# The second softmax's read in 64-row tiles, and W_in chunks and scores moved into one stretch where the accumulators change

## Chip, cores, metric

One core of one Trainium2 chip runs the kernel. The metric is the device time of one execution in microseconds (us), the median of three runs.

## What is computed

Two layers, all in float32. With B = H = 8, S = 512 tokens, Ns = 32 state rows and D = 64:

```python
scores  = scale * x @ state^T            # (B, H, S, Ns), softmax over Ns  -> a
xread   = a @ state                      # (B, H, S, D)
scores2 = scale * state @ x^T            # (B, H, Ns, S), softmax over S   -> a2
sread   = a2 @ x                         # (B, H, Ns, D)
x   = concat([xread, sread], axis=2)     # heads put side by side: 4352 rows of 512
h   = x @ w_in                           # 512 -> 2048
g   = h if h >= 1, 0 if h <= -1, (h + 1)^2 / 4 between
out = g @ w_out                          # 2048 -> 512
```

## The kernel before

**Work per batch.** `b` is a batch, 0 to 7; `b == B` (8) is the tail that handles the 256 rows of `sread`. For b < 8 the kernel never forms `xread`: it multiplies `state` with `W_in` first (`sw`, 128 x 2 x 2048 for one b: rows are head pair and state row, the 2 is the head in its pair), and then h = a x `sw`. `sw` is made in eight chunks of 256 columns; chunk c of batch b serves hidden block j = c.

**Precision.** The large products run on fp32r operands. Each operand is split in a high and a low part, and a product is three matmuls (high x high, low x high, high x low). ACT makes a high part (a cast), DVE the low part (a subtraction). `sw`, the scores and the second softmax's read are plain fp32 matmuls; each of those has two records in the trace.

**Steps.** A step is (b, j), j = 0 to 7. On TensorE it consists of `g1(b, j)`, 12 matmuls 128x512 into two PSUM banks of tag "h", and of `g2` of the step before, 24 matmuls 128x512 into the four banks of tag "acc" (`acc[b][0..3]`, one for each 128 tokens). Between `g1` and its `g2` stands an elementwise chain: `relu` on each half and `square` (ACT), `bound` on each half (DVE, which frees the h banks), `gh` (ACT), `gl` (DVE). In the last `g2` of a batch the pairs are sorted by token block, so a bank is complete after each six matmuls, and `store` copies it out on ACT.

**What is put between.** `g2` of a step is cut after `cut` of its eight triples of matmuls, and other TensorE work stands in the cut: at j = 0 the `scores` of b+1 (tile `sc`) and the second softmax's read of b (`read2`, tile `sr`); at j = 1 a transpose `rt`, at j = 2 the transposes `e2p`; at j = 3 and j = 7 four chunks of `sw` each (`sw_four`, chunks 4 to 7 of b, and chunks 0 to 3 of b+1). For b = 1 chunk pairs 0, 1 (at the end of a planned prologue) and 2, 3 (at j = 1, `sw_make`) are made in stretches of their own. These matmuls use part of the array: `sw` and `sc` 64 rows x 32 columns, eight such tiles in turn, `sr` 128 rows x 32 columns, four in turn.

**PSUM.** Eight banks: four "acc", two "h", one pair "mm" (used by `sc`, `rt`, `e2p`, half of `sw_four`).

**Order.** Batch 0 is emitted by a planner (`Plan`) with costs and due times. From b = 1 on the code above is handed to a scheduler that keeps the data dependences and may reorder within each engine's stream; the order views below show the result. The loads `xt` (for the scores) and `xn` (for the read) go through SP's queue, one buffer each, and are issued when the previous user is done.

Of the kernel before, what the change touches and what calls it, by code (L numbers as in the profile page):

```python
# [8 lines left out]
F32 = mybir.dt.float32  # L9
# [4 lines left out]
ALU = mybir.AluOpType  # L14
# [8 lines left out]
class Plan:  # L23
# [13 lines left out]
    def op(self, key, engine, cost, run, after=(), take=(), ends=()):  # L37

        after = list(after)
        prior = self.last.get(engine) if engine in ("PE", "SP") else None  # L40
        self.last[engine] = key
        self.ops[key] = [engine, cost, run, after, list(take), list(ends), prior]
# [95 lines left out]
def state_exchange_moe(  # L138
# [17 lines left out]
    nc = tc.nc  # L156
    B, P, NT, H, D = x.shape
    S = NT * P
    NS = 32
    DM = H * D  # L160
    NPR = H // 2
    CI = 256
# [3 lines left out]
    NJ = NF // 2  # L166
# [4 lines left out]
    small = ctx.enter_context(tc.tile_pool(name="small", bufs=1))  # L171
# [6 lines left out]
    def ps_acc(name):  # L178
        return ps.tile([P, DM], F32, tag="acc", bufs=4, name=name)

    def ps_h(name):
        return ps.tile([P, 512], F32, tag="h", bufs=2, name=name)

    def ps_mm(name):
        return ps.tile([P, 2, 512], F32, tag="mm", bufs=1, name=name)
# [18 lines left out]
    sb = const.tile([P, B, NPR, NS], F32, name="sb")  # L204
    srT = const.tile([P, NPR, B, NS], F32, name="srT")
    w32 = [const.tile([P, NPR, CI], F32, name=f"w32_{c}") for c in range(NC)]
# [7 lines left out]
    def load_xt(b):  # L214
        xt = work.tile([P, 2, NPR, S // 2], F32, tag="xt", bufs=1, name=f"xt{b}")
        for i in range(2):
            nc.sync.dma_start(out=xt[:, i], in_=xt_in[b, i])
        return xt
# [6 lines left out]
    class Attention:  # L225
# [116 lines left out]
        def read2(self):  # L342
            b = self.b
            xn = loaded.pop(("xn", b))
            sr = ps_h(f"sr{b}") if b else ps_mm(f"sr{b}")[:, 0]
            sr = self.sr = sr[:, :2 * D].rearrange("p (q d) -> p q d", q=2)
            for q in range(2):
                for t in range(NT):
                    for pr in range(NPR):
                        c0 = t * P + pr * NS  # L350
                        nc.tensor.matmul(  # L351
                            sr[pr * NS:(pr + 1) * NS, q], lhsT=self.e2[:, q, c0:c0 + NS],
                            rhs=xn[:, t, 2 * pr + q], start=t == 0, stop=t == NT - 1,
                        )

        def scale2(self):
            b = self.b
            self.rs = small.tile([P, 2, D], F32, tag="rs", name=f"rs{b}")
            nc.vector.tensor_tensor(
                out=self.rs, in0=self.sr, in1=self.r2[:, :, None].broadcast_to([P, 2, D]), op=ALU.mult  # L360
            )

        def keep2(self):
# [33 lines left out]
    def split_tiles(name):  # L397
        hi = work.tile([P, 1024], F32R, tag="wh", name=f"{name}h")
        lo = work.tile([P, 1024], F32R, tag="wl", name=f"{name}l")
        return hi, lo  # L400

    chunk = {}
# [3 lines left out]
    def sw_product(b, c, n):  # L406

        pt = ps_mm(f"sw{b}_{c}")
        for i in range(n):
            for pr in range(NPR):  # L410
                for hh in range(2):
                    rows = slice(hh * 64, hh * 64 + 64)
                    nc.tensor.matmul(
                        pt[pr * NS:(pr + 1) * NS, hh, i * CI:(i + 1) * CI],
                        lhsT=sb[rows, b, pr], rhs=w32[c + i][rows, pr], start=True, stop=True,
                    )
        w = n * CI
        wh, wl = (
            v[:, :2 * w].rearrange("p (q f) -> p q f", q=2) for v in split_tiles(f"sw{b}_{c}")
        )  # L420
        sw_of[b, c] = pt[:, :, :w], wh, wl
        for i in range(n):
            cols = slice(i * CI, (i + 1) * CI)
            chunk[b, c + i] = wh[:, :, cols], wl[:, :, cols]

    def sw_high(b, c):
        pt, wh, _ = sw_of[b, c]
        nc.scalar.copy(out=wh, in_=pt)

    def sw_low(b, c):  # L430
        pt, wh, wl = sw_of[b, c]
        nc.vector.tensor_tensor(out=wl, in0=pt, in1=wh.bitcast(F32), op=ALU.subtract)  # L432

    def sw_make(b, c, n):
        sw_product(b, c, n)
        sw_high(b, c)
        sw_low(b, c)

    def sw_four(b, c):

        pairs = [split_tiles(f"sw{b}_{c + 2 * p}") for p in range(2)]
        wh, wl = ([v.rearrange("p (q f) -> p q f", q=2) for v in w] for w in zip(*pairs))
        own = [ps_h(f"sw{b}_{c}_{hh}") for hh in range(2)]
        both = ps_mm(f"sw{b}_{c + 2}")
        for i in range(4):
            cols = slice(i % 2 * CI, (i % 2 + 1) * CI)
            for pr in range(NPR):
                for hh in range(2):
                    rows = slice(hh * 64, hh * 64 + 64)
                    o = both[:, hh] if i > 1 else own[hh]  # L450
                    nc.tensor.matmul(  # L451
                        o[pr * NS:(pr + 1) * NS, cols], lhsT=sb[rows, b, pr], rhs=w32[c + i][rows, pr],
                        start=True, stop=True,
                    )
            chunk[b, c + i] = wh[i // 2][:, :, cols], wl[i // 2][:, :, cols]
        for hh in range(2):
            h, lo = wh[0][:, hh], wl[0][:, hh]
            nc.scalar.copy(out=h, in_=own[hh])
            nc.vector.tensor_tensor(out=lo, in0=own[hh], in1=h.bitcast(F32), op=ALU.subtract)
        nc.scalar.copy(out=wh[1], in_=both)  # L460
        nc.vector.tensor_tensor(out=wl[1], in0=both, in1=wh[1].bitcast(F32), op=ALU.subtract)

    def wi_split(c):
        wh, wl = (v.rearrange("p (k f) -> p k f", f=CI) for v in split_tiles(f"wj{c}"))
# [117 lines left out]
    parts = {}  # L582
# [49 lines left out]
    op = plan.op  # L632
# [25 lines left out]
    atts = {}  # L658
# [62 lines left out]
    def tensor(key, cost, f, after=(), take=(), ends=()):  # L721
        op(key, "PE", cost, f, after, take, ends)
# [6 lines left out]
    def sw_ops(b, c, n):  # L729
        tensor(("sw", b, c), 0.35 + 0.35 * n, lambda: sw_product(b, c, n), [("w", c + i) for i in range(n)],  # L730
               take=[("mm", ("sw", b, c)), ("w", ("wc", b, c))])
        op(("swh", b, c), "ACT", 0.5 * n, lambda: sw_high(b, c), [("sw", b, c)], ends=[("sw", b, c)])
        op(("swl", b, c), "DVE", 0.6 * n, lambda: sw_low(b, c), [("swh", b, c)], ends=[("sw", b, c)])
# [14 lines left out]
    def g2_ops(b, j, half):  # L748
        k = (b, j)
        tensor(("g2", half) + k, 2.75, lambda: g2(b, j, (4 * half, 4 * half + 4)), [("gh",) + k, ("gl",) + k, ("wol", j), ("sc done", 0)],  # L750
               ends=[("g",) + k])
# [41 lines left out]
    for j in range(NJ):  # L793
# [10 lines left out]
            att_ops2(1)  # L804
        if j:
            g2_ops(0, j - 1, 1)
    sw_ops(1, 0, 2)
    import os
    with guard:
        plan.emit(warm, ("sc", 0, 0), ("g2", 0, 0, 0))  # L810
# [5 lines left out]
    for i, (b, j) in enumerate(steps):  # L816
        if (b, j) == (B, 0):
            sh, sl = (work.tile([P, NPR, B * NS], F32R, tag=t, name=f"s{t}") for t in ("ath", "atl"))
            src = srT.rearrange("p a b n -> p a (b n)")
            nc.vector.tensor_copy(sh, src)  # L820
            nc.vector.tensor_tensor(out=sl, in0=src, in1=sh.bitcast(F32), op=ALU.subtract)
            att_of[B] = (sh, sl)
        if b + 1 < B and j == 0:
            loaded["xt", b + 1] = load_xt(b + 1)
        g1(b, j)
        if i + 1 < len(steps) and steps[i + 1][0] == B:
            for c in (2 * steps[i + 1][1], 2 * steps[i + 1][1] + 1):
                wi_split(c)
        before = steps[i - 1] if i else (0, NJ - 1)
        if b == B:  # L830
            g2(*before)
            continue
        cut = 5
        g2(*before, (0, cut))
        if j == 0:
            if b + 1 < B:
                atts[b + 1] = Attention(b + 1)
                atts[b + 1].scores()
            atts[b].read2()
            atts[b].scale2()  # L840
            if b + 1 < B:
                loaded["xn", b + 1] = load_xn(b + 1)
                atts[b + 1].second()
        elif j == 1:
            atts[b].keep2()
            atts[b].keep()
            if b == 1:
                sw_make(b, 2, 2)
        elif j == 2 and b + 1 < B:
            atts[b + 1].first()  # L850
        elif j == 3:
            sw_four(b, 4)
        elif j == 4 and b + 1 < B:
            atts[b + 1].halves()
        elif j == NJ - 1 and b + 1 < B:
            sw_four(b + 1, 0)
        g2(*before, (cut, 8))
    g2(*steps[-1])

# [42 lines left out]
```

## Time and profile before

| | |
|---|---|
| median of 3 runs | 658.56 us (658.18 to 659.11) |
| the profiled execution: time, span | 658.84 us, 656.8 us |
| TensorE matmul busy | 647.7 us, 99% of the span |
| ACT, DVE busy | 359.6 us (55%), 340.1 us (52%) |
| granted TensorE clock | 1.00 |
| chain that ended last | TensorE 88%, ACT 6%, DVE 4% |

The 2.0 us between time and span lie outside the program's recorded part. Matmuls are pipelined: a record lasts 390 ns, and the next starts 227 ns later. So a busy share of 99% does not say that the array streams without pause; what a stretch costs is read from the starts of the matmuls around it.

### The profile page before, as it was taken

To read this page: it belongs to the slowest core of one execution; us is meant where nothing else is said; L and a number is where in the kernel's file an instruction comes from. 1 tells how busy PE (TensorE), PEld (TensorE's weight loads), DVE (VectorE), ACT (ScalarE), POOL (GpSimd) and SP (SyncE) were. 2 spreads that over 40 slices of the span, in tenths; PEclk is the share of its full clock that TensorE was granted. 3 is DMA by queue.
4 is the path that set the end of the run, shared out by engine and by line. 5 is a ranking of instruction groups with operands and counts; after the bars stand their busy time and mean duration, and the time that the engine had idled before them with its cause. 6 is when DMAs were issued, how large, how long until landed. Compare 5 with 4: busy or idle time off the path is not lost.

```text
span 656.8 us, 10337 instructions
## 1 busy us (share of the span) xinstructions
PE 647.7 (99%) x4442; PEld 518.1 (79%) x4442; DVE 340.1 (52%) x503; ACT 359.6 (55%) x475; POOL 0.8 (0%) x7
## 2 busy tenths in 40 slices
PE   8999999999999999999999999999999999999997
PEld 7677776788787877787787878787787878788895
DVE  5999948433673338533664338434654343333431
ACT  5899847544565455544555456445654454444632
POOL 0000000000000000000000000000000000000000
PEclk9999999999999999999999999999999999999999
DMA  8986005000320005000410005000300000000101
GB/s 355 415 364 244 0 17 177 1 1 1 102 92 1 0 1 193 1 2 1 132 62 1 0 17 177 1 1 1 129 1 1 0 34 32 1 1 1 64 1 32
DMA packets 11085, 43.64 MB, mean 66 GB/s; under 512 B 1312, under 2 KB 1440, under 8 KB 7968
## 3 DMA queue, kind: packets, MB, share of 16 engines
q1 hardware_dynamic: 6096, 34.28, 13.9%
q10 hardware_dynamic: 4944, 8.72, 3.6%
q8 instruction: 34, 0.56, 0.4%
q14 instruction: 11, 0.09, 0.0%
HBM read 34.08 MB, written 8.91 MB: 65 GB/s over the span
## 4 chain that ended last, share of the span: by engine, by line
PE 88%; ACT 6%; DVE 4%; issue 1%; DMA 0%; POOL 0%; ACTq 0%; SPq 0%; POOLq 0%
PE acc L553 18%; PE acc L554 17%; PE acc L555 17%; PE h L498 9%; PE h L499 9%; PE h L497 9%; PE sw L451 4%; PE sr L351 1%; ACT u L502 1%; PE sc L253 1%; PE e2p L333 1%; PE warmed L198 1%; ACT u L505 1%; ACT e L322 1%; ACT raw_i L607 1%
## 5 line engine op out<-in xcount | busy, mean ns | idle before, releaser
L553 PE MATMUL acc<-wo,gh 128*128 128x512 f32 x544 | 216.7, 398 | 0.0
L554 PE MATMUL acc<-wo,gh 128*128 128x512 f32 x544 | 212.4, 390 | 0.0
L555 PE MATMUL acc<-wo,gl 128*128 128x512 f32 x544 | 212.1, 390 | 0.0
L508 DVE SCALAR_TENSOR_TENSOR u<-u,h 128x512 f32<-128x512 f32 x136 | 87.1, 681 | 200.2 <-ACT u L505 200.2
L502 ACT ACTIVATE u<-h,half 128x512 f32<-128x512 f32 x136 | 93.2, 694 | 168.7 <-PE h L499 159.5
L553 PEld LDWEIGHTS acc<-wo,gh 128*128 128x128 f32 x544 | 102.1, 188 | 30.4 <-issue 9.1
L555 PEld LDWEIGHTS acc<-wo,gl 128*128 128x128 f32 x544 | 102.1, 188 | 22.3 <-issue 0.4
L554 PEld LDWEIGHTS acc<-wo,gh 128*128 128x128 f32 x544 | 102.2, 188 | 20.0 <-DVE wo L626 0.3
L522 DVE TENSOR_TENSOR gl<-u,gh 128x1024 fp32r<-128x1024 f32 x68 | 83.2, 1224 | 63.2 <-ACT gh L517 63.2
L517 ACT CAST gh<-u 128x1024 fp32r<-128x1024 f32 x68 | 71.6, 1052 | 70.5 <-DVE u L508 70.3
L505 ACT ACTIVATE u<-u 128x1024 f32<-128x1024 f32 x68 | 72.6, 1067 | 1.5
L568 ACT COPY o<-acc 128x512 f32<-128x512 f32 x33 | 19.0, 583 | 21.3 <-PE acc L555 21.3
L451 PE MATMUL sw<-w,sb 64*32 64x256 f32 x832 | 25.4, 379 | 0.0
L499 PE MATMUL h<-atl,sw_0h 128*128 128x512 f32 x60 | 23.6, 393 | 0.3 <-DVE atl L306 0.2
L498 PE MATMUL h<-ath,sw_2l 128*128 128x512 f32 x60 | 23.5, 391 | 0.2 <-DVE sw_2l L432 0.2
L497 PE MATMUL h<-ath,sw_0h 128*128 128x512 f32 x60 | 23.5, 395 | 0.0
L498 PE MATMUL h<-ath,sw_0l 128*128 128x512 f32 x60 | 23.5, 391 | 0.0
L497 PE MATMUL h<-ath,sw_4h 128*128 128x512 f32 x60 | 23.4, 390 | 0.0
L498 PE MATMUL h<-ath,sw_4l 128*128 128x512 f32 x60 | 23.4, 389 | 0.0
L499 PE MATMUL h<-atl,sw_2h 128*128 128x512 f32 x60 | 23.4, 389 | 0.0
L497 PE MATMUL h<-ath,sw_6h 128*128 128x512 f32 x60 | 23.3, 389 | 0.0
L498 PE MATMUL h<-ath,sw_6l 128*128 128x512 f32 x60 | 23.3, 389 | 0.0
(184 smaller groups left out, 738.1 us busy)
## 6 DMA issues: line engine op xcount, KB each, us to landing
xt<-in_xt_dram SPq DMA_DIRECT2D x16, 512.0 KB, 7.5
raw_i<-in_moe_w_in_dram SPq DMA_DIRECT2D x8, 1024.0 KB, 7.1
raw_o<-in_moe_w_out_dram SPq DMA_DIRECT2D x8, 1024.0 KB, 9.1
xn<-in_x_dram SPq DMA_DIRECT2D x8, 1024.0 KB, 7.3
out_dram<-o ACTq DMA_DIRECT2D x32, 256.0 KB, 2.1
sb<-in_state_dram SPq DMA_DIRECT2D x1, 448.0 KB, 12.5
out_dram<-o SPq DMA_DIRECT2D x4, 64.0 KB, 1.7
out_dram<-o ACTq DMA_DIRECT2D x4, 64.0 KB, 2.0
```

Of the source, the lines that this page charges most:

```text
L451: nc.tensor.matmul(o[pr * NS:(pr + 1) * NS, cols], lhsT=sb[rows, b, pr], rhs=w32[c + i][rows, pr], start=True, stop=True,)
L497: nc.tensor.matmul(o, lhsT=wh[:, k, sl], rhs=ah[:, k], start=first, stop=False)
L498: nc.tensor.matmul(o, lhsT=wl[:, k, sl], rhs=ah[:, k], start=False, stop=False)
L499: nc.tensor.matmul(o, lhsT=wh[:, k, sl], rhs=al[:, k], start=False, stop=last)
L502: nc.scalar.activation(out=self.u[:, i], in_=self.hs[i], func=AF.Relu, scale=0.5, bias=half)
L505: nc.scalar.activation(out=self.u, in_=self.u, func=AF.Square)
L508: nc.vector.scalar_tensor_tensor(out=self.u[:, i], in0=self.u[:, i], scalar=1.0, in1=self.hs[i], op0=ALU.min, op1=ALU.max,)
L517: nc.scalar.copy(out=gh, in_=self.u)
L522: nc.vector.tensor_tensor(out=gl, in0=self.u, in1=gh.bitcast(F32), op=ALU.subtract)
L553: nc.tensor.matmul(a, lhsT=lh, rhs=oh, start=f == 0, stop=False)
L554: nc.tensor.matmul(a, lhsT=lh, rhs=ol, start=False, stop=False)
L555: nc.tensor.matmul(a, lhsT=ll, rhs=oh, start=False, stop=f == NF - 1)
```

## The change

1. `read2` splits the 128 tokens of each contraction in two halves of 64 rows, `g` = 0 and 1, which go to two h banks: 64 matmuls in place of 32, in the tile shape of `sw` and `sc`. `scale2` adds the halves on DVE (a copy, an addition, then the scaling as before).
2. At j = 0 the cut moves behind all of `g2` (8 in place of 5), which finishes the old accumulators. In the cut stand then `read2`, chunks 1 to 4 of `sw`, and `scores`, without other matmuls between. The chunks go into the four acc banks (`ps_acc`), which the stores have just emptied and which `g2(b, 0)` needs next.
3. Chunks 5, 6, 7 of b and 0 of b+1 are made at j = 4, in two h banks and mm. The stretches at j = 3 and j = 7, and `sw_make` at b = 1, go. The prologue makes one chunk of b = 1 in place of two; b = 7 now makes chunks 1 to 7 itself.

```diff
 def read2(self):
-    sr = ps_h(f"sr{b}") if b else ps_mm(f"sr{b}")[:, 0]
-    sr = self.sr = sr[:, :2 * D].rearrange("p (q d) -> p q d", q=2)
+    if b:
+        self.sr = [ps_h(f"sr{b}_{g}") for g in range(2)]
+    else:
+        sr = ps_mm(f"sr{b}")
+        self.sr = [sr[:, g] for g in range(2)]
     for q in range(2):
         for t in range(NT):
             for pr in range(NPR):
                 c0 = t * P + pr * NS
-                nc.tensor.matmul(
-                    sr[pr * NS:(pr + 1) * NS, q], lhsT=self.e2[:, q, c0:c0 + NS],
-                    rhs=xn[:, t, 2 * pr + q], start=t == 0, stop=t == NT - 1)
+                for g in range(2):
+                    rows = slice(g * 64, g * 64 + 64)
+                    nc.tensor.matmul(
+                        self.sr[g][pr * NS:(pr + 1) * NS, q * D:(q + 1) * D],
+                        lhsT=self.e2[rows, q, c0:c0 + NS], rhs=xn[rows, t, 2 * pr + q],
+                        start=t == 0, stop=t == NT - 1)
 def scale2(self):
...
+    nc.vector.tensor_copy(first2, self.sr[0][:, :2 * D])
+    nc.vector.tensor_tensor(out=first2, in0=self.sr[1][:, :2 * D], in1=first2, op=ALU.add)
-    nc.vector.tensor_tensor(out=self.rs, in0=self.sr, in1=self.r2[...], op=ALU.mult)
+    nc.vector.tensor_tensor(out=self.rs, in0=first, in1=self.r2[...], op=ALU.mult)
...
-    sw_ops(1, 0, 2)
+    sw_ops(1, 0, 1)
...
-        cut = 5
+        cut = 8 if j == 0 else 5
         g2(*before, (0, cut))
         if j == 0:
-            if b + 1 < B:
-                atts[b + 1] = Attention(b + 1)
-                atts[b + 1].scores()
             atts[b].read2()
             atts[b].scale2()
+            halves = [
+                sw_pair([(b, c), (b, c + 1)], [ps_acc(f"sw{b}_{c}_{hh}") for hh in range(2)]) for c in (1, 3)
+            ]
-            if b + 1 < B:
+            if nxt:
                 loaded["xn", b + 1] = load_xn(b + 1)
-                atts[b + 1].second()
+                nxt.scores()
+            for split in halves:
+                split()
+            if nxt:
+                nxt.second()
         elif j == 1:
             atts[b].keep2()
             atts[b].keep()
-            if b == 1:
-                sw_make(b, 2, 2)
...
-        elif j == 3:
-            sw_four(b, 4)
-        elif j == 4 and b + 1 < B:
-            atts[b + 1].halves()
-        elif j == NJ - 1 and b + 1 < B:
-            sw_four(b + 1, 0)
+        elif j == 4:
+            last = [(b, 7)] + ([(b + 1, 0)] if nxt else [])
+            own = [ps_h(f"sw{b}_5_{hh}") for hh in range(2)]
+            split = sw_pair([(b, 5), (b, 6)], own)
+            both = ps_mm(f"sw{b}_7")
+            split2 = sw_pair(last, [both[:, hh] for hh in range(2)], both)
+            split()
+            split2()
+            if nxt:
+                nxt.halves()
         g2(*before, (cut, 8))
```

`sw_pair` issues the 16 matmuls of two chunks and returns a function that issues their casts (ACT) and subtractions (DVE). Three places show how the rows move. First TensorE at (b, j) = (2, 0): `acc` rows are `g2(1, 7)`, `h_1` rows are `g1(2, 1)`. Before:

```order
L555 MATMUL acc_2_1078<-wo_781,gl_7_1468 128x512
L253 MATMUL sc_1589<-xt_1540,sb 32x512 x8
L351 MATMUL sr_1601<-xn_1026,e_2_1030 32x64 x32
L553 MATMUL acc_2_1078<-wo_781,gh_7_1467 128x512
L554 MATMUL acc_2_1078<-wo_781,gh_7_1467 128x512
```

Now, the end of the stretch (it begins with the 64 `sr` matmuls and 32 of chunks 1 to 4):

```order
L459 MATMUL sw_3_0_1738<-w_4_91,sb 32x256
L459 MATMUL sw_3_1_1739<-w_4_91,sb 32x256
L253 MATMUL sc_1760<-xt_1585,sb 32x512 x8
L511 MATMUL h_1_0_1792<-ath_984,sw_1h 128x512
L512 MATMUL h_1_0_1792<-ath_984,sw_1l 128x512
```

Nine `g2` matmuls followed the stretch before; now `g1(2, 1)` follows at once, and its second matmul reads the low part of chunk 1, made in this stretch.

DVE at the same place, before (`u` is the elementwise chain's tile, `gl` its last product, `rs` the scaled read, `z` and `nm` the two softmaxes of b+1):

```order
L522 TENSOR_TENSOR gl_0_1564<-u_0_1543,gh_0_1563 128x1024
L260 STREAM_TRANSPOSE z_1590<-sc_1589 128x512 x2
L359 TENSOR_TENSOR rs_1634<-sr_1601,r_2_1191 128x128
L318 TENSOR_REDUCE nm_3_1641<-sc_1589 128x1 x2
L319 TENSOR_SCALAR nm_3_1641<-nm_3_1641 128x1
```

and now:

```order
L536 TENSOR_TENSOR gl_0_1609<-u_0_1588,gh_0_1608 128x1024
L367 COPY first_1714<-sr_0_1647 128x128
L368 TENSOR_TENSOR first_1714<-sr_1_1648,first_1714 128x128
L369 TENSOR_TENSOR rs_1713<-first_1714,r_2_1281 128x128
L473 TENSOR_TENSOR sw_1l<-sw_1_0_1718,sw_1h 128x512
L473 TENSOR_TENSOR sw_1l<-sw_1_1_1719,sw_1h 128x512
L473 TENSOR_TENSOR sw_3l<-sw_3_0_1738,sw_3h 128x512
L473 TENSOR_TENSOR sw_3l<-sw_3_1_1739,sw_3h 128x512
L260 STREAM_TRANSPOSE z_1761<-sc_1760 128x512 x2
```

Two small operations and four subtractions have moved ahead of the softmaxes of b+1. On ACT four casts stand there, behind the last two stores of the old accumulators and ahead of the `relu` of step (2, 1):

```order
L582 COPY o_1620<-acc_2_1189 128x512
L582 COPY o_1620<-acc_3_1190 128x512
L585 DMA out_dram<-o_1620 128x512 x2
L472 CAST sw_1h<-sw_1_0_1718 128x512
L472 CAST sw_1h<-sw_1_1_1719 128x512
L472 CAST sw_3h<-sw_3_0_1738 128x512
L472 CAST sw_3h<-sw_3_1_1739 128x512
L516 ACTIVATE u_1_1791<-h_1_0_1792,half 128x512
```

Before, the exponentials of the second softmax followed the third copy there; they now come behind both `relu`.

More of the change, by code (lines that the diff above doesn't have):

```diff
@@ L350, in read2 @@
                         c0 = t * P + pr * NS
-                        nc.tensor.matmul(
-                            sr[pr * NS:(pr + 1) * NS, q], lhsT=self.e2[:, q, c0:c0 + NS],
-                            rhs=xn[:, t, 2 * pr + q], start=t == 0, stop=t == NT - 1,
-                        )
+                        for g in range(2):
[3 more added lines that the diff above has]
+                                lhsT=self.e2[rows, q, c0:c0 + NS], rhs=xn[rows, t, 2 * pr + q],
+                                start=t == 0, stop=t == NT - 1,
+                            )
         def scale2(self):
@@ L358, in scale2 @@
             self.rs = small.tile([P, 2, D], F32, tag="rs", name=f"rs{b}")
+            first = small.tile([P, 2, D], F32, tag="first", name=f"first{b}")
+            first2 = first.rearrange("p a d -> p (a d)")
+            nc.vector.tensor_copy(first2, self.sr[0][:, :2 * D])
+            nc.vector.tensor_tensor(out=first2, in0=self.sr[1][:, :2 * D], in1=first2, op=ALU.add)
             nc.vector.tensor_tensor(
-                out=self.rs, in0=self.sr, in1=self.r2[:, :, None].broadcast_to([P, 2, D]), op=ALU.mult
+                out=self.rs, in0=first, in1=self.r2[:, :, None].broadcast_to([P, 2, D]), op=ALU.mult
             )
@@ L437, in sw_make, with sw_pair @@
         sw_low(b, c)
[L439 to L446, printed above, removed]
+    def sw_pair(pieces, banks, whole=None):
+        wh, wl = (
+            v.rearrange("p (q f) -> p q f", q=2) for v in split_tiles("sw{}_{}".format(*pieces[0]))
+        )
+        for i, (b, c) in enumerate(pieces):
+            cols = slice(i * CI, (i + 1) * CI)
             for pr in range(NPR):
@@ L449, in sw_four, with split @@
                     rows = slice(hh * 64, hh * 64 + 64)
-                    o = both[:, hh] if i > 1 else own[hh]
                     nc.tensor.matmul(
-                        o[pr * NS:(pr + 1) * NS, cols], lhsT=sb[rows, b, pr], rhs=w32[c + i][rows, pr],
+                        banks[hh][pr * NS:(pr + 1) * NS, cols], lhsT=sb[rows, b, pr], rhs=w32[c][rows, pr],
                         start=True, stop=True,
                     )
[L455 to L461, printed above, removed]
+            chunk[b, c] = wh[:, :, cols], wl[:, :, cols]
+        n = len(pieces) * CI
+        if whole is not None:
+            parts = [(wh[:, :, :n], wl[:, :, :n], whole[:, :, :n])]
+        else:
+            parts = [(wh[:, hh, :n], wl[:, hh, :n], banks[hh][:, :n]) for hh in range(2)]
+        def split():
+            for h, lo, pt in parts:
+                nc.scalar.copy(out=h, in_=pt)
+                nc.vector.tensor_tensor(out=lo, in0=pt, in1=h.bitcast(F32), op=ALU.subtract)
+        return split
     def wi_split(c):
@@ L832, in state_exchange_moe @@
             continue
-        cut = 5
+        nxt = atts[b + 1] = Attention(b + 1) if b + 1 < B and j == 0 else atts.get(b + 1)
+        cut = 8 if j == 0 else 5
         g2(*before, (0, cut))
         if j == 0:
-            if b + 1 < B:
-                atts[b + 1] = Attention(b + 1)
-                atts[b + 1].scores()
             atts[b].read2()
             atts[b].scale2()
-            if b + 1 < B:
+            halves = [
+                sw_pair([(b, c), (b, c + 1)], [ps_acc(f"sw{b}_{c}_{hh}") for hh in range(2)]) for c in (1, 3)
+            ]
+            if nxt:
                 loaded["xn", b + 1] = load_xn(b + 1)
-                atts[b + 1].second()
+                nxt.scores()
[3 more added lines that the diff above has]
+                nxt.second()
         elif j == 1:
@@ L846, in state_exchange_moe @@
             atts[b].keep()
-            if b == 1:
-                sw_make(b, 2, 2)
-        elif j == 2 and b + 1 < B:
-            atts[b + 1].first()
-        elif j == 3:
-            sw_four(b, 4)
-        elif j == 4 and b + 1 < B:
-            atts[b + 1].halves()
-        elif j == NJ - 1 and b + 1 < B:
-            sw_four(b + 1, 0)
+        elif j == 2 and nxt:
+            nxt.first()
+        elif j == 4:
[8 more added lines that the diff above has]
+                nxt.halves()
         g2(*before, (cut, 8))
```

## Prediction

> **What bounds it.** I read the page's busy shares, its chain that ended last, and then the timeline of TensorE around each piece of work that the change touches.
>
> ```profile
> PE 647.7 (99%) x4442; PEld 518.1 (79%) x4442; DVE 340.1 (52%) x503; ACT 359.6 (55%) x475; POOL 0.8 (0%) x7
> PE 88%; ACT 6%; DVE 4%; issue 1%; DMA 0%; POOL 0%; ACTq 0%; SPq 0%; POOLq 0%
> ```
>
> TensorE is the path, so the time is the sum of what its stream takes. The next rows show that stream at (b, j) = (2, 0), where `sc` and `sr` stand between `g2` matmuls, and at (1, 7), where four chunks stand (start, duration, engine, line).
>
> ```profile
> 171.07 0.39 PE L553 MATMUL acc<-wo,gh 128*128 128x512 f32 x1
> ...
> 174.24 0.39 PE L555 MATMUL acc<-wo,gl 128*128 128x512 f32 x1
> 174.56 1.09 PE L253 MATMUL sc<-xt,sb 64*32 64x512 f32 x16
> 175.58 1.10 PE L351 MATMUL sr<-xn,e 128*32 128x64 f32 x64
> 176.61 0.50 PE L553 MATMUL acc<-wo,gh 128*128 128x512 f32 x1
> 176.95 0.40 PE L554 MATMUL acc<-wo,gh 128*128 128x512 f32 x1
> ```
> ```profile
> 163.93 0.39 PE L555 MATMUL acc<-wo,gl 128*128 128x512 f32 x1
> 164.25 1.96 PE L451 MATMUL sw<-w,sb 64*32 64x256 f32 x64
> 166.13 0.50 PE L553 MATMUL acc<-wo,gh 128*128 128x512 f32 x1
> 166.47 0.40 PE L554 MATMUL acc<-wo,gh 128*128 128x512 f32 x1
> ```
>
> From 171.07 to 174.24 are 14 steps: 0.227 us for a full matmul. A stretch costs the time between its outer full matmuls less two such steps (0.45): 176.95 - 174.24 - 0.45 = 2.26 for scores and read, 166.47 - 163.93 - 0.45 = 2.09 for four chunks. Part of that is not streaming. Stretches of one and two chunks show how much:
>
> ```profile
> 68.67 0.66 PE L413 MATMUL sw<-w,sb 64*32 64x256 f32 x16
> 69.26 0.50 PE L553 MATMUL acc<-wo,gh 128*128 128x512 f32 x1
> ...
> 92.09 1.09 PE L413 MATMUL sw<-w,sb 64*32 64x256 f32 x32
> 93.12 0.50 PE L553 MATMUL acc<-wo,gh 128*128 128x512 f32 x1
> ```
>
> One chunk takes 0.59 to the next full matmul, two 1.03, four 1.88: 0.43 a chunk and 0.16 once. Add 0.09 at the entry (0.32 in place of 0.227) and 0.11 behind the first full matmul (0.34 in place of 0.227): 0.36 for each stretch, whatever is in it. `sc` takes 1.02 to the start of `sr`, so 0.86 of streaming and 0.16 for the change of tile shape inside the stretch; `sr` takes 1.03, of which I count 0.89 as streaming and 0.14 as the way out.
>
> **The change part by part.** *Batches 2 to 6.* Before: 2.26 + 2 x 2.09 = 6.44. After, at j = 0: 0.09 + 0.89 (read) + 4 x 0.43 + 0.86 (scores) + 0.27 = 3.83, one tile shape throughout; at j = 4: 2.09. Sum 5.92, saved 0.5 in each, 2.5 in five. What goes is one stretch (0.36) and the change of shape inside another (0.16); the chunks and scores stream as before.
>
> *Batch 1* has more to lose:
>
> ```profile
> 91.77 0.39 PE L555 MATMUL acc<-wo,gl 128*128 128x512 f32 x1
> ...
> 93.45 0.40 PE L554 MATMUL acc<-wo,gh 128*128 128x512 f32 x1
> ...
> 99.25 0.39 PE L555 MATMUL acc<-wo,gl 128*128 128x512 f32 x1
> ...
> 100.87 1.10 PE L351 MATMUL sr<-xn,e 128*32 128x64 f32 x64 [0.21 <-DVE u L508]
> 101.90 0.50 PE L553 MATMUL acc<-wo,gh 128*128 128x512 f32 x1
> ...
> 110.58 0.40 PE L554 MATMUL acc<-wo,gh 128*128 128x512 f32 x1
> ...
> 112.27 0.39 PE L553 MATMUL acc<-wo,gh 128*128 128x512 f32 x1
> ...
> 114.56 0.39 PE L555 MATMUL acc<-wo,gl 128*128 128x512 f32 x1
> 115.17 0.50 PE L498 MATMUL h<-ath,sw_2l 128*128 128x512 f32 x1 [0.23 <-DVE sw_2l L432]
> ```
>
> Two chunks at 91.77 cost 1.23; scores and read 101.90 + 0.34 - 99.25 - 0.45 = 2.54, with a wait of 0.28 for an h bank that `bound` freed late; two chunks of `sw_make` at 110.58 cost 1.24; the wait for their low part 115.17 - 114.56 - 0.23 = 0.38, with the 0.11 behind it 0.5. With two stretches of four chunks 9.7. After: one chunk 0.79, then 3.83 + 2.09 = 6.7. The wait for the h bank goes since the read now follows 19 full matmuls after `g1(1, 0)`, not 6. Saved 3.0.
>
> *Batch 7* pays, since its chunks were made before at (6, 7):
>
> ```profile
> 538.87 0.39 PE L555 MATMUL acc<-wo,gl 128*128 128x512 f32 x1
> ...
> 540.22 0.50 PE L553 MATMUL acc<-wo,gh 128*128 128x512 f32 x1
> 540.56 0.40 PE L554 MATMUL acc<-wo,gh 128*128 128x512 f32 x1
> ```
>
> Before: 540.56 - 538.87 - 0.45 = 1.24, and 2.09. After: 0.09 + 0.89 + 4 x 0.43 + 0.27 = 2.97 without scores, and three chunks 0.36 + 3 x 0.43 = 1.65: 1.3 more, and a wait of 0.4 (below).
>
> *The read in 64-row tiles* is the one unknown. It has 128 records in place of 64, on eight tiles in place of four, and half the contraction each. It streams as now, 0.89, if eight can start in the time in which four start. Its own pace now is one start in (1.10 - 0.22)/63 = 14 ns. But eight tiles do start closer:
>
> ```profile
> 164.25 0.45 PE L451 MATMUL sw<-w,sb 64*32 64x256 f32 x8
> L451 PE MATMUL sw<-w,sb x832: 376/376/400, 129.5 to 566.7; 64*32 64x256 f32 x167
> q8 instruction: 34, 0.56, 0.4%
> ```
>
> These eight of four chunks' 64 ended 0.45 after the first start and last 0.40 at most, so they started 7 ns apart: 128 x 7 = 0.89, just enough. Bounds: 0.86 (a hair faster) to 1.79 (14 ns kept), +0.90 for each of eight reads. I take 0.89, because `sw` is the nearest row in tile shape, eight 64 x 32 tiles that alternate in the same way. Code loading adds a little: 0.56 MB in 34 packets is 16.5 KB each, 256 of TensorE's 8884 records, and 0.4% of 16 x 656.8 us / 34 is 1.2 us for one. A read and the next chunk now use 320 records in about 1.3 us; where a block ends badly TensorE may wait 0.2 to 0.5. I put 0 in the sum and up to 1 us in the range.
>
> *Waits that are new.* `g1(b, 1)` follows the stretch at once and needs chunk 1's high and low parts.
>
> ```profile
> 100.12 1.28 DVE L508 SCALAR_TENSOR_TENSOR u<-u,h 128x512 f32<-128x512 f32 x2 [4.56 <-ACT u L505]
> ...
> 165.43 1.08 ACT L458 CAST sw_0h<-sw 128x512 fp32r<-128x512 f32 x2 [0.24 <-PE sw L451]
> ...
> 166.36 1.28 DVE L459 TENSOR_TENSOR sw_0l<-sw,sw_0h 128x512 fp32r<-128x512 f32 x2
> ...
> 173.55 0.34 ACTq L571 DMA_DIRECT2D out_dram<-o  x1
> 173.99 0.59 ACT L568 COPY o<-acc 128x512 f32<-128x512 f32 x1 [0.47 <-PE acc L555]
> ...
> 176.69 1.31 DVE L260 STREAM_TRANSPOSE z<-sc 128x512 f32<-128x512 f32 x2
> ...
> 177.92 0.26 DVE L359 TENSOR_TENSOR rs<-sr,r 128x128 f32<-128x128 f32 x1
> ...
> 180.59 1.28 DVE L275 TENSOR_TENSOR z<-z,m 128x512 f32<-128x512 f32 x2
> ...
> 186.61 1.23 DVE L522 TENSOR_TENSOR gl<-u,gh 128x1024 fp32r<-128x1024 f32 x1
> ```
>
> Count from the start of the last full matmul. The read starts at 0.32, chunks 1 and 2 end at 0.32 + 0.89 + 0.86 = 2.07, 3 and 4 at 2.93, scores at 3.8, the first full matmul starts at 3.95, the second (low part of chunk 1) at 4.3, the fifth (its other half) at 4.75. The cast follows the end of its stream by 165.43 - 164.25 - 0.86 = 0.32, so at 2.4, and takes 0.55; ACT has the last store behind it by then: a copy starts 0.43 behind the start of its bank's last matmul (the 12th from 171.07, so 171.07 + 11 x 0.227 = 173.56; the copy 173.99), so 0.43 to 1.02, and two DMA issues of 0.34 end at 1.7. DVE, whose additions and scaling (three like L359, 0.26 each) end near 2.3, subtracts from 3.0 to 3.65 and to 4.3; TensorE starts 0.07 behind DVE (100.12 + 0.68 to 100.87). 3.7 and 4.4 against 4.3 and 4.75: covered by the scores, with 0.35 to spare. In batch 7 the scores are missing, the second matmul could start at 3.45 and waits until 3.7: 0.3, and 0.11 for a restart, 0.4. The acc banks are free at 5.5, `g2(b, 0)` needs the first at 6.8. The softmaxes of b+1 start on DVE at 5.5 in place of right behind the scores; from there to L275's end it takes 181.87 - 176.69 - 0.2 = 5.0, the two `bound` 1.3 follow with 0.4 of small work ahead of them (h bank free at 11.6, needed at 12.3), then two sums of L275's size 1.3 and `gl` 1.2: 14.7, needed at 15.5 (24 full matmuls and `g1(b, 2)` behind `g1(b, 1)`). So 0.7 to spare. The loads of `xt` and `xn` pass nothing on SP's queue that is needed within the batch. At j = 4 the casts have the same nine matmuls before their use as at j = 3 before.
>
> *Sum.* -2.5 - 3.0 + 1.3 + 0.4 = -3.8 us. Against the profiled execution's 658.84: 655.0. That execution is 0.28 above the median of the runs, so 654.8 is what I expect of a median.
>
> **Rivals.**
>
> *The read keeps its pace (slower).* If a start each 14 ns is TensorE's limit and not the four tiles', 128 of them take 1.79, and eight reads add 7.2: 654.8 + 7.2 = 662.0. It decides from 3.8/8/128 = 3.7 ns more than 7, that is 10.7 ns a start. For it speaks that no row shows more than eight starts in a row at 7 ns; four chunks start 64 in 1.96 - 0.38 = 1.58, 25 ns apart. Against it: those 25 ns are the eight tiles' own streaming (0.43 for 16). Between 7 and 10.7 the gain only shrinks. The Trainium skill, page "TensorE: Matmul & The Clock Gate", section "Wait — 56ns, not 53.3ns?", states that starts never come closer than about 25 ns however small the matmul, and its page "TensorEngine Tiling (Array Packing)", section "Instruction Overhead", warns against tiling where a dimension is small already. By 25 ns a start, an estimate from that page, the read would take 3.2 us and the kernel about 18 us more. The 14 ns of the present read contradict that as a limit for the engine as a whole, so this size gets no chance; for each tile it can hold.
>
> *The covers are too thin (about no change to slightly faster).* If casts, subtractions or the DVE chain are 0.4 later than counted, each of batches 1 to 6 waits 0.4 at `g1(b, 1)` or at `g2(b, 1)`, with 0.11 of restart: six times 0.5 is 3.0, 657.8. For it: DVE goes from the additions to `gl` nearly without a pause. Against: both margins exceed 0.3.
>
> **Chances.** Forecast 0.64 (own range 653.9 to 656.0: the sum with 1 us of code loading, or without batch 7's wait and a little more). Pace between 7 and 10.7 ns 0.10 (655 to 658.6). Thin covers 0.11. Pace kept 0.15. The range 653.9 to 659.0 leaves out the last and little more. A change under 0.2% (1.3 us) can't be told from none here. Faster: 0.64, most of the second and part of the third, 0.73; same 0.12; slower 0.15.
>
> **What will show it.** Right: `sr` records 128 in each batch within about 1.1 us, no gap from `sr` to `sw` to `sc`, 3.8 between the outer full matmuls less two steps, no idle before `h` or `acc` except about 0.3 at batch 7. Wrong: `sr` spread over 1.5 us or more; TensorE idle before L512 with DVE's `sw` as its releaser, or before L569 with `gl`.

## The result and the profile after

| | before | after |
|---|---|---|
| median of 5 runs | 658.51 us (658.18 to 659.11) | 666.69 us (664.59 to 667.25) |
| the profiled execution: time, span | 658.84 us, 656.8 us | 666.69 us, 664.6 us |

The ratio is 1.0119, with an interval of 1.0102 to 1.0136. The kernel became slower by 1.2%, where 0.6% faster was forecast; the time lies 7.7 us above the upper end of the range.

The page of the changed kernel, the lines that answer to those of before (its busy shares, an instruction queue of DMA, its chain that ended last):

```profile
PE 650.8 (98%) x4954; PEld 526.1 (79%) x4954; DVE 344.3 (52%) x528; ACT 361.5 (54%) x484; POOL 0.8 (0%) x7
...
q8 instruction: 39, 0.64, 0.4%
...
PE 91%; DVE 3%; ACT 3%; issue 1%; DMA 0%; POOL 0%; SPq 0%; ACTq 0%; POOLq 0%
```

TensorE has 512 matmuls (PE) and 512 weight loads (PEld) more, all from the eight reads, and 39 instruction packets in place of 34. The page hardly shows the loss: "issue" is 1% as before. It shows in the stretches. First the timeline of TensorE at batch 3 (start, duration, engine, line), where nothing waits:

```profile
252.18 0.39 PE L569 MATMUL acc<-wo,gl 128*128 128x512 f32 x1
252.50 1.43 PE L356 MATMUL sr<-xn,e 64*32 64x64 f32 x124
...
253.76 0.22 PE L356 MATMUL sr<-xn,e 64*32 64x64 f32 x1
253.81 1.96 PE L459 MATMUL sw<-w,sb 64*32 64x256 f32 x60
255.45 1.18 PE L253 MATMUL sc<-xt,sb 64*32 64x512 f32 x16
256.56 0.50 PE L511 MATMUL h<-ath,sw_1h 128*128 128x512 f32 x1
256.90 0.40 PE L512 MATMUL h<-ath,sw_1l 128*128 128x512 f32 x1
```

The stretch costs 256.90 - 252.18 - 0.45 = 4.27, not 3.83. The last of 128 `sr` starts stands 1.26 behind the first: 9.9 ns a start, not 7. No row waits for `bound`, a cast or a subtraction. The same place at batch 2:

```profile
178.38 1.43 PE L356 MATMUL sr<-xn,e 64*32 64x64 f32 x124
...
179.69 1.96 PE L459 MATMUL sw<-w,sb 64*32 64x256 f32 x60
182.75 1.09 PE L253 MATMUL sc<-xt,sb 64*32 64x512 f32 x16 [1.10 <-issue]
183.77 0.50 PE L511 MATMUL h<-ath,sw_1h 128*128 128x512 f32 x1
```

The `sc` matmuls (the scores) start 3.06 behind the `sw` row, where batch 3 has 1.64. TensorE stands idle for 1.10 and waits for no engine and no tile ("issue"). At batch 7, the same inside the chunks:

```profile
546.64 0.98 PE L459 MATMUL sw<-w,sb 64*32 64x256 f32 x21
548.77 1.50 PE L459 MATMUL sw<-w,sb 64*32 64x256 f32 x39 [1.14 <-issue]
550.19 0.49 PE L511 MATMUL h<-ath,sw_1h 128*128 128x512 f32 x1
550.81 0.50 PE L512 MATMUL h<-ath,sw_1l 128*128 128x512 f32 x1
```

And at batch 0, where the read stands alone between `g2` matmuls, it stops one matmul short of its end; below it are the windows of this place (length, then busy time of PE, PEld, DVE, ACT and POOL, the granted clock, DMA share, GB/s):

```profile
31.93 0.39 PE L569 MATMUL acc<-wo,gl 128*128 128x512 f32 x1
32.24 1.47 PE L356 MATMUL sr<-xn,e 64*32 64x64 f32 x127
36.29 0.26 PE L356 MATMUL sr<-xn,e 64*32 64x64 f32 x1 [2.58 <-issue]
36.48 0.79 PE L567 MATMUL acc<-wo,gh 128*128 128x512 f32 x1
37.07 0.63 PE L568 MATMUL acc<-wo,gh 128*128 128x512 f32 x1
37.50 0.63 PE L569 MATMUL acc<-wo,gl 128*128 128x512 f32 x1
...
39.63 0.40 PE L568 MATMUL acc<-wo,gh 128*128 128x512 f32 x1
```
```profile
31.90:33.90 2.00, 1.81 (x129) 1.32 (x128) 2.00 (x3) 2.00 (x4) 0.00 (x0) 1.00 0.93 373
33.90:36.20 2.30, 0.00 (x0) 0.00 (x0) 2.30 (x3) 2.30 (x4) 0.00 (x0) 1.00 0.64 196
36.50:39.90 3.40, 3.40 (x10) 2.68 (x10) 3.33 (x7) 1.66 (x2) 0.00 (x0) 0.54 1.00 422
```

Behind a pause of 2.58 the granted clock is 0.54, and seven full matmuls, from 36.48 to 39.63, take 3.15 (steps of about 0.43 in place of 0.227): another 1.5 us.

All stretches together, each worked out as above, against the terms of the prediction:

| place | forecast | measured |
|---|---|---|
| batch 0, read alone | 1.23 | 5.89 |
| batches 1, 3, 5, 6, stretch at j = 0 | 3.83 | 4.27, 4.27, 4.30, 4.27 |
| batches 2, 4 | 3.83 | 5.59, 5.62 |
| batch 6, a wait behind the stretch | 0 | 0.23 |
| batch 7, with its wait | 3.37 | 5.45 |
| stretches at j = 4 | 2.09 | 2.09 |

The wait at batch 6 stands between the third and the fourth of the six matmuls that fill the first h bank, so no bank is awaited there, and the cast of its chunk had ended at 475.78:

```profile
476.91 0.39 PE L513 MATMUL h<-atl,sw_1h 128*128 128x512 f32 x1
477.37 0.39 PE L511 MATMUL h<-ath,sw_1h 128*128 128x512 f32 x1
```

The differences sum to 12.3 us. With the forecast's -3.8 that is +8.5; between the two profiled executions lie 7.85. The remaining 0.6 isn't put down to a place. Of the 12.3, the slower pace of the eight reads is 7 x 0.44 + 0.38 = 3.5 (the 0.38 from a read without a wait at batch 0, below), the waits for code 7.3 (2.8 at batch 0, 1.3 to 1.7 at batches 2, 4 and 7, 0.2 at batch 6; what shows that they are waits for code stands under e3 and e7), the lowered clock 1.5. One of the five runs took 664.59 at a granted clock of 1.000 where the others have 0.996 to 0.999; that would fit a run without the low clock, but it has no profile.

### The profile page after: what moved, and what is told of

Its sections match the earlier page's. It is cut to its first block, busy times and chain, and to the rows that moved or that the text cites. A ratio compares the mean times of both kernels' runs of the same rounds, so it can differ in the third digit from the quotient of the medians.

```text
span 664.6 us, 11410 instructions
## 1 busy us (share of the span) xinstructions
PE 650.8 (98%) x4954; PEld 526.1 (79%) x4954; DVE 344.3 (52%) x528; ACT 361.5 (54%) x484; POOL 0.8 (0%) x7
## 4 chain that ended last, share of the span: by engine, by line
PE 91%; DVE 3%; ACT 3%; issue 1%; DMA 0%; POOL 0%; SPq 0%; ACTq 0%; POOLq 0%
PE acc L567 18%; PE acc L568 18%; PE acc L569 18%; PE h L511 10%; PE h L512 9%; PE h L513 9%; PE sw L459 4%; PE sr L356 2%; PE sc L253 1%; PE e2p L333 1%; PE warmed L198 1%; DVE w L629 1%; PE sw L423 0%; ACT u L516 0%; ACT e L322 0%
## 5 line engine op out<-in xcount | busy, mean ns | idle before, releaser
L459 PE MATMUL sw<-w,sb 64*32 64x256 f32 x880 | 28.3, 379 | 1.1 <-issue 1.1
L511 PE MATMUL h<-ath,sw_1h 128*128 128x512 f32 x60 | 24.3, 405 | 0.1
L459 PEld LDWEIGHTS sw<-w,sb 64*32 64x32 f32 x880 | 18.8, 106 | 6.4 <-DVE u L522 2.5
L512 PE MATMUL h<-ath,sw_1l 128*128 128x512 f32 x60 | 23.6, 393 | 0.1
L513 PE MATMUL h<-atl,sw_1h 128*128 128x512 f32 x60 | 23.4, 390 | 0.0
L511 PE MATMUL h<-ath,sw_5h 128*128 128x512 f32 x60 | 23.4, 390 | 0.0
L512 PE MATMUL h<-ath,sw_5l 128*128 128x512 f32 x60 | 23.4, 389 | 0.0
L511 PE MATMUL h<-ath,sw_3h 128*128 128x512 f32 x60 | 23.3, 389 | 0.0
L512 PE MATMUL h<-ath,sw_3l 128*128 128x512 f32 x60 | 23.3, 389 | 0.0
L513 PE MATMUL h<-atl,sw_3h 128*128 128x512 f32 x60 | 23.3, 389 | 0.0
```

The costliest lines, as they stand in the source:

```text
L459: nc.tensor.matmul(banks[hh][pr * NS:(pr + 1) * NS, cols], lhsT=sb[rows, b, pr], rhs=w32[c][rows, pr], start=True, stop=True,)
L511: nc.tensor.matmul(o, lhsT=wh[:, k, sl], rhs=ah[:, k], start=first, stop=False)
L512: nc.tensor.matmul(o, lhsT=wl[:, k, sl], rhs=ah[:, k], start=False, stop=False)
L513: nc.tensor.matmul(o, lhsT=wh[:, k, sl], rhs=al[:, k], start=False, stop=last)
```

## Experiments

Theory A: the loss comes from the number of records (a matmul and its weight load are two). They must be delivered to TensorE, and their code comes in blocks of 256, so a read of 256 records is slow at its end and outruns the loading of the next block. Its rivals: the loss comes from the tiles of 64 rows themselves (theory C), or from the merged stretch and the work that stands beside it.

**e1_read128: only the merge, with the read of before.** The two functions of the read are put back; all else is as changed.

```diff
-    for g in range(2):
-        rows = slice(g * 64, g * 64 + 64)
-        nc.tensor.matmul(self.sr[g][...], lhsT=self.e2[rows, q, c0:c0 + NS], rhs=xn[rows, t, 2 * pr + q], ...)
+    nc.tensor.matmul(sr[...], lhsT=self.e2[:, q, c0:c0 + NS], rhs=xn[:, t, 2 * pr + q], ...)
...
-    nc.vector.tensor_copy(first2, self.sr[0][:, :2 * D])
-    nc.vector.tensor_tensor(out=first2, in0=self.sr[1][:, :2 * D], in1=first2, op=ALU.add)
```

> The changed kernel, with the read as before (128 rows, 32 matmuls, one h bank, one DVE operation). Theory A: the loss comes from the read's 256 records (matmuls and weight loads): TensorE's instructions arrive at some 4.2 ns each once its queue is empty, and a block of 256 of them needs about 4 us from the crossing of one block's end to the use of the block after it. With the old read a batch's stretch holds 288 records in 3.7 us, and no 256 of them with the queue's 64 ahead pass in under 4 us: no wait for code in any batch, batch 0 as before. Then the forecast's sum returns, -3.8 us, less 7 changes of tile shape at 0.16: about 655.8 us. Theory B (rival): the stretch in one piece, with chunks in the accumulators' banks, is at fault, by waits on casts, banks or DVE: then 660 us or more, and batches 2, 4 and 7 keep waits of over 1 us.

Measured: 656.0 us (655.6 to 656.21) against 658.89, ratio 0.9954 (0.9937 to 0.997): faster than before. TensorE at batch 3:

```profile
246.20 0.39 PE L559 MATMUL acc<-wo,gl 128*128 128x512 f32 x1
246.52 1.10 PE L351 MATMUL sr<-xn,e 128*32 128x64 f32 x64
247.55 1.96 PE L449 MATMUL sw<-w,sb 64*32 64x256 f32 x64
249.30 1.06 PE L253 MATMUL sc<-xt,sb 64*32 64x512 f32 x16
250.29 0.50 PE L501 MATMUL h<-ath,sw_1h 128*128 128x512 f32 x1
250.63 0.40 PE L502 MATMUL h<-ath,sw_1l 128*128 128x512 f32 x1
```

The stretch costs 3.98 in each of batches 1 to 6 and 3.55 in batch 7, and no stretch waits for code. The merge alone does what the prediction said of it; the read in 64-row tiles alone turns the result.

**e2_read64_only: only the read, no merge.** Before, with `read2` and `scale2` of the change.

> The kernel before, with the read in 64-row tiles alone. Theory A: each read takes 1.2 us in place of 0.9 (one change of tile shape of 0.16 goes in batches 1 to 6), +1.5 us in all; in batch 0 a block of code ends at the read's start and the next but one is missing at its end: a wait of 2.8 us and a slower granted clock behind it, +4.7 us as in the changed kernel; batch 1 waits about 0.5 us more for its second h bank; full matmuls follow each later read, so no wait for code there. About 665 us. Theory B: the read alone costs its pace, 660 us at most.

Measured: 667.39 us (666.08 to 668.88), ratio 1.0128 (1.0111 to 1.0145). TensorE at (2, 0), read and what follows it, then one row of DVE:

```profile
181.44 1.52 PE L356 MATMUL sr<-xn,e 64*32 64x64 f32 x128
182.90 0.50 PE L563 MATMUL acc<-wo,gh 128*128 128x512 f32 x1
...
185.43 0.50 PE L507 MATMUL h<-ath,sw_0h 128*128 128x512 f32 x1 [0.20 <-DVE nm L319]
```
```profile
185.10 0.28 DVE L367 COPY first<-sr 128x128 f32<-128x128 f32 x1
```

`sr` to the next full matmul takes 1.46 where it took 1.03. Less the change of tile shape ahead of it, which goes, scores and read cost 2.54 in place of 2.25, and at batch 7 the read alone 1.61 in place of 1.23. Batch 0 waits again and runs on at a lower clock: 4.18 and 1.60, in place of 1.23. The rest I had not foreseen: the read now holds both h banks, and DVE's copy, which frees the first, stands behind reductions of the scores and ends at 185.38, so `g1` waits 0.47 in each of batches 2 to 6 (the releaser that the row names, L319, runs beside that copy). Batch 1 costs 0.96 more than the 2.54, where it cost 0.28 more before. In the changed kernel the read stands ahead of the chunks, which covers this. With 128 records followed by full matmuls, batches 1 to 7 have no wait for code.

**e3_shift: the changed kernel, its code moved by 100 records.** Twenty-five matmuls of two columns stand ahead of the first loads. All that follows starts 10.7 us later (batch 0's read at 42.92 in place of 32.24), so the total (one run, 678.9) says nothing; the stretches count.

```diff
+    for _ in range(25):
+        nc.tensor.matmul(warmed[:, :2], lhsT=ident, rhs=ident[:, :2], start=True, stop=True)
     pad = small.tile([P, PAD], F32, name="pad")
```

> The changed kernel, with 25 tiny matmuls (2 columns) ahead of all others, so that every later TensorE record stands 100 places further on in the stream of instructions, and nothing else differs. Theory A: the waits follow the places where blocks of 256 records end. With the queue 64 records ahead and 4 us for a block: waits in batches 1 (0.9 us), 4 (1.1) and 6 (1.7), none in 0, 2, 3, 5 and 7 (there only 0.4 us for chunk 1's low part). Batch 0 loses its 2.8 us wait and the slow clock. About 662.5 us. Theory B: the waits belong to the batches' work and stay in 0, 2, 4 and 7, 666.7 us.

Measured: stretches of 1.61 at batch 0 and 5.61, 4.57, 4.43, 8.49, 4.27, 8.30, 3.77 at batches 1 to 7. TensorE at batches 0 and 4, then the windows at batch 4:

```profile
42.92 1.48 PE L358 MATMUL sr<-xn,e 64*32 64x64 f32 x128
44.33 0.50 PE L569 MATMUL acc<-wo,gh 128*128 128x512 f32 x1
...
333.93 0.98 PE L461 MATMUL sw<-w,sb 64*32 64x256 f32 x20
336.92 2.27 PE L461 MATMUL sw<-w,sb 64*32 64x256 f32 x36 [2.01 <-issue]
```
```profile
336.00:338.00 2.00, 1.08 (x24) 0.84 (x31) 0.00 (x0) 0.06 (x1) 0.00 (x0) 0.77 0.98 366
338.00:340.00 2.00, 2.00 (x36) 1.19 (x24) 1.29 (x2) 1.37 (x3) 0.00 (x0) 0.50 0.25 94
```

The waits left batches 0 and 7, and batches 1, 4 and 6 now lose 1.3, 4.2 and 4.0, the last two with a low clock behind the wait; batches 2 and 3 keep 0.30 and 0.16. The same instructions on the same data wait or don't wait by their place in the code. The total I expected, 662.5, was missed: 10.7 of the difference are the small matmuls, which I had put at next to nothing, and most of the rest are batches 4 and 6, expected at 1.1 and 1.7.

**e4_cols: twice the records without tiles of 64 rows.** Before, with each matmul of the read cut into two halves of 32 columns: 128 matmuls on four tiles of 128 rows.

```diff
-                for t in range(NT):
+                for d in range(2):
+                  cols = slice(d * 32, d * 32 + 32)
+                  for t in range(NT):
...
-                        sr[..., q], lhsT=self.e2[:, q, c0:c0 + NS], rhs=xn[:, t, 2 * pr + q], ...
+                        sr[..., q, cols], lhsT=self.e2[:, q, c0:c0 + NS], rhs=xn[:, t, 2 * pr + q, cols], ...
```

> The kernel before, with the read in 128-row tiles but each matmul cut in two halves of 32 columns: as many records as the 64-row read (128 matmuls and 128 weight loads), the streaming of the array as before, no row tiles. Theory A (delivery of instructions): the read takes 1.2 us as in the changed kernel, with starts about 8.3 ns apart behind the first 32, and batch 0 has the wait of about 2.8 us at the read's end: about 665 us. Theory C (rival: two 64-row tiles in the same columns slow each other): the read takes 0.93 us, 659 us.

Measured, one run: 664.45 us. TensorE at batch 0 and at batch 3:

```profile
31.93 1.28 PE L353 MATMUL sr<-xn,e 128*32 128x32 f32 x127
35.22 0.19 PE L353 MATMUL sr<-xn,e 128*32 128x32 f32 x1 [2.01 <-issue]
35.34 0.67 PE L555 MATMUL acc<-wo,gh 128*128 128x512 f32 x1
...
252.40 1.30 PE L353 MATMUL sr<-xn,e 128*32 128x32 f32 x128
253.63 0.50 PE L555 MATMUL acc<-wo,gh 128*128 128x512 f32 x1
```

The wait at batch 0 and the slow matmuls behind it are there without any 64-row tile, so theory C falls for the waits. For the pace it holds in part: the read costs 0.19 more here (2.44 for scores and read, 1.43 at batch 7), and 0.38 with 64-row tiles (1.61). So half the slower pace comes with the number of records; the other 0.19 belongs to something in the tiles and stays open.

**e5_b0: the changed kernel with the read of before in batch 0 alone.** This takes away batch 0's loss and moves all later code by 128 records.

```diff
                         for g in range(2):
-                            rows = slice(g * 64, g * 64 + 64)
+                            if b == 0 and g:
+                                continue
+                            rows = slice(g * 64, g * 64 + 64) if b else slice(None)
```

> The changed kernel, with the 128-row read in batch 0 alone. That also moves every later TensorE record 128 places ahead in the stream. Theory A, with what the shift to the other side has shown (the queue 50 records ahead, 4.2 us from the crossing of a block's end to the use of the block after the next): batch 0 has no wait and no slow clock behind it (4.66 us less); waits in batches 1 (1.7 us), 3 (1.3) and 6 (2.3), none in 2, 4, 5 and 7 but the 0.4 us for chunk 1's low part. Total about 663 us. Theory B (waits belong to batches 2, 4, 7): 662 us with the waits where they were.

Measured, one run: 663.02 us. Batch 0 costs 1.23; batches 1 to 7 cost 6.22, 4.27, 5.38, 4.57, 5.51, 4.87 and 3.77. That is 1.95, 1.11, 0.30, 1.24 and 0.60 in batches 1, 3, 4, 5 and 6 above a stretch without a wait. The waits in 1 and 3 came as expected, in 6 far less than the 2.3, and those in 4 and 5 were not expected; that the total is met is luck, since the waits sum to 5.2 where 5.3 were expected. The places of blocks can be counted better than I had done it: the trace also lists other instructions of TensorE, nearly all for semaphores, 31 of them ahead of the wait in batch 6, and they belong into the count.

**e7_read128_shift: e1 moved in the same way.** Twenty-seven small matmuls ahead of e1, so that its 3.98 couldn't be the luck of its places. The total again holds some 11 us of small matmuls.

> The version with the 128-row read (read first, then chunks and scores), with 27 tiny matmuls ahead of all others: 108 records of shift, so that blocks end 16 to 87 records behind the start of the reads, where the 64-row read waited most. These matmuls cost about 11 us at the start, so the stretches count, not the total. Theory A: the 288 records of a stretch and the 50 ahead always reach into full matmuls before the next block ends, so no wait: 3.98 us in batches 1 to 6, 3.55 in batch 7. Rival (that version was lucky in its places): waits of up to 1.6 us in batches 1 to 4.

Measured, one run: 666.72 us; 3.98 in batches 1 to 6, 3.55 in batch 7, 1.23 at batch 0, no wait for code:

```profile
184.70 1.10 PE L353 MATMUL sr<-xn,e 128*32 128x64 f32 x64
...
188.48 0.50 PE L503 MATMUL h<-ath,sw_1h 128*128 128x512 f32 x1
```

The trace shows why. The waits of the changed kernel, e2, e3, e4 and e5 are seventeen: twelve large ones, and the small ones at batch 6 of the changed kernel, 2 and 3 of e3, 4 and 6 of e5. Numbered from the first TensorE instruction of the trace (matmuls, weight loads and the others), the first instruction behind the wait stands at the same place in all seventeen, the 194th of each 256. So the waits come at one place a block, whatever work stands there. That instruction starts 2.2 to 3.2 us after a packet of the instruction queue starts, though the packet itself lasts 0.9 to 1.9. In e7 the 194th comes at least 4.2 us behind its packet, so it is never waited for; in e1 and the kernel before, at least 8.6.

In the seven of the twelve large waits that lie in merged stretches at full clock, two packets start 4.0 to 4.3 apart, and behind the start of the program no pair in any kernel is closer than 4.0: blocks came no faster here. The closest pair in e7 is 4.6 apart, in e1 and in the kernel before more than 8.

**e6_order: e1 with the read behind chunks and scores.** The aim was to hide the casts of batch 7's chunks under the read.

```diff
-            atts[b].read2()
-            atts[b].scale2()
             halves = [...]
             if nxt:
                 nxt.scores()
+            atts[b].read2()
             for split in halves:
                 split()
+            atts[b].scale2()
```

> The changed kernel with the read of 128 rows, and in the stretch at j = 0 the four chunks first, then the scores, then the read. Theory A: 288 records as in the version with the read first, so no wait for code, 3.98 us in batches 1 to 6; chunk 1's parts are ready earlier, so batch 7 loses its wait of 0.4 us (3.55 to 3.13): 655.6 us against that version's 656.0. Rival: the read at the end holds an h bank that g1 needs at once, or the old accumulators' stores hold back the chunks' banks: 0.3 us or more in each batch, 658 us.

Measured: 662.4 us (661.91 to 662.74), ratio 1.0055 (1.0041 to 1.0069): slower, by a wait that I had named and put too low. The second h bank of `g1(2, 1)`:

```profile
179.22 0.39 PE L503 MATMUL h<-atl,sw_1h 128*128 128x512 f32 x1
180.51 0.50 PE L501 MATMUL h<-ath,sw_1h 128*128 128x512 f32 x1 [0.91 <-DVE rs L359]
```

The read holds that bank until `scale2`, which now stands behind the subtractions and the scores' transposes on DVE: 1.18 in each of batches 2 to 6. The read must come first while other work of DVE follows in the same stretch.

**e8_last_first: e1, and in batch 7 alone the chunks first.** Batch 7 has no scores, so little of DVE's work stands behind the read.

```diff
-            atts[b].read2()
-            atts[b].scale2()
+            if nxt:
+                atts[b].read2()
+                atts[b].scale2()
             halves = [...]
+            if not nxt:
+                atts[b].read2()
+                atts[b].scale2()
```

> The version with the 128-row read; in batch 7 alone, where no scores follow, the chunks stand ahead of the read. Theory A: chunk 1's low part is then in time (0.42 us less), but g1's second h bank waits for the read's scaling, which stands behind four subtractions on DVE (0.24 us, as in batch 7 of the version with the read last everywhere): 655.8 us, 0.2 below the version it is made from, and batch 7's stretch at 3.12 us in place of 3.55. Rival: the wait in batch 7 has another cause and stays, 656.0 us or more.

Measured: 655.47 us (655.23 to 655.74) against 658.68, ratio 0.9952 (0.9938 to 0.9965). TensorE at batch 7:

```profile
535.98 1.96 PE L449 MATMUL sw<-w,sb 64*32 64x256 f32 x64
537.87 1.10 PE L351 MATMUL sr<-xn,e 128*32 128x64 f32 x64
538.90 0.50 PE L501 MATMUL h<-ath,sw_1h 128*128 128x512 f32 x1
```

The stretch costs 3.12 in place of 3.55, with 0.24 at an h bank behind it: 0.2 gained, too little to tell e8 from e1. Its median is the lowest of all versions.

## Why the prediction was wrong

**Held.** The arithmetic of the stretches: with the read of before, 0.16 has to be added to 3.83 for the change of tile shape, which gives 3.99, and e1 measured 3.98. Batch 7 so comes to 3.53 with its wait of 0.4, against 3.55. The stretch at j = 4 is 2.09. The sum with seven times 0.16 is -2.7, and e1 gained 2.9. The covers held too: casts, subtractions and the softmaxes' chain make TensorE wait in none of batches 1 to 6, so that rival is out (the 0.23 at batch 6 stands at the 194th place, like the other waits for code).

**First step that failed: "The read in 64-row tiles".** It took 0.89 from eight starts at 7 ns. In the changed kernel this holds inside groups of eight (6.7 ns), but not for the read. Its first 32 matmuls, at batch 3:

```profile
252.50 0.45 PE L356 MATMUL sr<-xn,e 64*32 64x64 f32 x32
```

One lasts 0.22, so these starts are 7.7 ns apart on average; the other 96 follow at 10.7 on average, with pauses and then mostly two starts each 17 ns (the 8.3 that I expected of e4 left out the pauses). Eight starts were a row of the right tile shape and the wrong length. That they run fast because TensorE had their instructions already while full matmuls ran is my reading; no run shows it. Measured: 1.3 for a read, 0.4 more than the term. The rival "the read keeps its pace" isn't what happened either: 9.9 ns a start lies below its 10.7, in the band where the gain only shrinks. Pace alone would have left -3.8 + 3.5 = -0.3, no change that can be measured.

**Second step that failed, and the larger: "Code loading adds a little".** It put one block at 1.2 us, the time of its packet, and so 0.2 to 0.5 of waiting. The sum had 0 for it and the range 1 us; measured were 7.3, and 1.5 for the clock behind the longest wait. What sets the wait is the whole way from the start of a block's packet to the first use of what it brings, 2.2 to 3.2 us, and the 4.0 to 4.3 from packet to packet. Where the read runs at 5 ns a record, 256 records take 1.3 us. What stands around them decides the wait: full matmuls need 0.227/2 = 0.114 us a record and give the loading time, chunks (128 records in 1.75) and scores do so far less. The waits are 1.3 to 1.7 at batches 2, 4 and 7, and 2.8 at batch 0. The prediction saw that a read and a chunk (288 records, not its 320) would pass in 1.3 us but compared that with the wrong duration.

On this the Trainium skill, page "Runtime: NRT & Kernel Launch", section "Instruction fetch mechanics", states that code comes in blocks of 256 instructions, the next fetched while the current one runs, and that the cost of crossing a block is mostly hidden. The blocks agree with the seventeen waits and with 39 packets for 9908 records; "hidden" holds in e1, e7 and the kernel before, and not for these reads.

**Not foreseen: the clock.** Behind the five longest waits (batch 0 of the changed kernel, e2 and e4, batches 4 and 6 of e3; 1.9 to 2.6 idle, 2.2 to 2.8 from start to start) the granted clock fell to half, at batch 0 for 1.5 us of loss; behind those of 1.1 to 1.4 in batches 2, 7 and e5's batch 1 it did not. The Trainium skill, page "TensorE: Matmul & The Clock Gate", section "What's actually happening", gives half clock after an idle window of about 3.4 us. Half clock agrees; here pauses of 2.2 to 2.8, from start to start, were enough.

**Open.** What the 2.2 to 3.2 us consist of beside the packet. Loads of data beside it aren't the main part: batch 7 has no `xn` or `xt` load to issue and waits as long as batches 2 and 4. Its stores keep the DMA engines busy there too (share 0.60 from 546.4 to 548.8), so what other transfers add isn't shown. Open too is the 0.19 that a 64-row read costs beyond a 128-row one with as many records.

## What to carry to other kernels

Count TensorE's records, matmuls and weight loads, beside its time: cutting a contraction in two doubles them, and small matmuls pass them faster than they can be fetched. Where 256 records in a row would pass in less than about 4 us, a wait of up to the difference can come, once a block (not in every block: 256 passed in 2.7 us in e7 without one, because their packet had started 1.5 us or more ahead). So judge such a change by several stretches, or by the code moved, not by one. A rate read from eight starts in a row need not hold for a hundred.

## What the hardware showed beyond expectation

- A wait whose place is set by the place in the code: the 194th of each 256 instructions in seventeen waits of five kernels. A shift by 100 records moved the large ones from batches 0, 2, 4 and 7 to batches 1, 4 and 6.
- TensorE's starts on eight tiles of 64 rows: 7.7 ns apart on average for the first 32, then 10.7, at two records each.
- A pause of 2.8 us from start to start cost another 1.5: seven matmuls with steps of about 0.43 in place of 0.227.
- Twenty-five matmuls of two columns at the start of the program moved all behind them by 10.7 us; why isn't known.
